# First solve of a delta-rule and mixture kernel: beta over squared norms, first evictions on two engines, and idle products cut from 18 long to 46 short

## The chip, the cores and the metric

The kernel runs on one core of one Trainium2 chip. The metric is device time in microseconds (us) of one execution, as the median of several. Durations of single instructions are in nanoseconds (ns) where so marked. The engines are TensorE (PE, with its weight loads as a row of its own, PEld), VectorE (DVE), ScalarE (ACT), GpSimd (POOL) and SyncE (SP, which issues most of the DMAs).

## The reference

For each of 4 x 8 heads a 48 x 48 state is carried over 768 positions. The output of that, as rows of 384, goes through a two-layer product with a clipped square between the layers.

```python
k_n = k / (np.linalg.norm(k, axis=-1, keepdims=True) + 1e-06)
for t in range(S):
    kt, vt, bt = (k_n[:, :, t], v[:, :, t], beta[:, :, t, None])
    y[:, :, t] = np.einsum('bhd,bhde->bhe', q[:, :, t], state)
    v_old = np.einsum('bhde,bhd->bhe', state, kt)
    state = state + bt[:, :, :, None] * np.einsum('bhd,bhe->bhde', kt, vt - v_old)
...
h = x @ w_in
g = np.where(h >= 1, h, np.where(h <= -1, 0.0, (h + 1) ** 2 / 4))
out = g @ w_out
```

## The kernel before, in words

The 768 positions are cut into 12 chunks of 64. Two chunks make a stage G. Inside a chunk the recurrence becomes a triangular system, so each stage needs the products of keys with keys (Gram matrices), the norms of the keys, the inverse of a triangular matrix (the solve), and then a chain of products that carries the state.

The chunks of stage 0 come first, and nothing can be overlapped with an earlier stage there: this is the front. Lines 679 to 713 write its order out by hand. `gram_k(g)` (L231) makes the Gram matrices of chunk g in two PSUM banks (L237) and returns its eviction, which copies the two banks to SBUF (L241). `lanes(G)` (L298) is a generator whose steps are run one at a time: two steps copy 32-column blocks side by side (L304, and L306 for stage 1), one step transposes them on DVE so that each partition holds one small system (L317), one step makes the norms and `gm` = beta / norm^2 (L319 to L327), and one multiplies the matrix by `gm` (L338) and transposes the norms (L340). `norms` (L277) takes a square root on ACT (L281) and does a Newton step on DVE (L282 to L285); `gm` then takes a reciprocal and two multiplications (L322 to L324). `solve(0)` (L343) is 15 steps of a multiplication and a subtraction on DVE (L355, L357). `unlanes(0)` (L386) multiplies by `gm` and transposes back (L391, L394, L396) into the tile XT. `scale_v` (L288) multiplies the values by the norms (L292).

PE meanwhile runs what it can: `place_beta` (L151, one product at L153), the key-query products (`gram_q`, L250), the Gram matrices of chunks 3 and 2, and between them products of a tile of zeros that nobody reads (`dense`, L163; L165). `dense(IDLE)` at L690 is the last of these: 18 products of 512 columns in the type fp32r, just ahead of the second `place_beta` (L705) and of `merge16_a` (L401, products at L405, evicted by ACT at L412), which needs the XT of `unlanes(0)`. Then come `merge16_b` (L419, subtracted and transposed by DVE at L424 and L425), `merge32` (L436, then L451 on ACT, L438, L443 on ACT), and the chain: `chain_u` (L508), `chain_y` (L539, L541; evicted at L556 and L561) and `chain_d` (L607). `stage` (L647) takes the strings in FRONT (L30), which put other work between: F one idle product, A and D steps of unpacking weights on ACT (L189, L205) and DVE (L195, L201, L208), L a step of `lanes(1)`, s a step of `scale_v(0)`, w a weight load (L124).

From L861 on a loop over (stage, weight tile) runs the two large products (`up`, L738, and `down`, L753), with the work of later stages between them.

All products of the type fp32 show as two weight loads and two products each in the trace; those of type fp32r show as one of each.

Of the kernel before, what the change touches and what calls it, by code (L numbers as in the profile page):

```python
# [7 lines left out]
F32 = mybir.dt.float32  # L8
F32R = mybir.dt.float32r
I32 = mybir.dt.int32  # L10
AF = mybir.ActivationFunctionType
ALU = mybir.AluOpType
# [7 lines left out]
DF = 2048  # L20
FT = DF // 128
WARM = 8
IDLE = 18
DENSE = (8, 4, 8, 10)
HALF = 6
PASSES = ((0, 0), (0, 1), (1, 0))
# [14 lines left out]
def delta_rule_moe(ctx: ExitStack, tc: tile.TileContext, kqa, kqb, kv, beta, w, out):  # L41
# [14 lines left out]
    nc = tc.nc  # L56
# [5 lines left out]
    P = 128  # L62
# [4 lines left out]
    sb = ctx.enter_context(tc.tile_pool(name="sb", bufs=2))  # L67
# [3 lines left out]
    K, KE, GE, Q, KV, XB, RAW, WT = {}, {}, {}, {}, {}, {}, {}, {}  # L71
# [9 lines left out]
    def half(x):  # L81
        return slice(x * H, x * H + H)
# [46 lines left out]
    beta_sb = const.tile([P, NS, 32], F32, name="beta_sb")  # L129
# [16 lines left out]
    for c0, base, step, n in ((0, -H, -C, NP), (NP, -C - H - NP, C, NP), (C, -C, C, H)):  # L146
        x = perm[:, 0:C].rearrange("c (a f l) -> c a f l", f=2, l=H)[:, :, :, c0:c0 + NP] if c0 < C else perm[:, C:P].rearrange("c (a f l) -> c a f l", f=2, l=H)
# [3 lines left out]
    def place_beta(n0, n1):  # L151
        b_ps = ps.tile([P, NS, 32], F32, **acc())
        nc.tensor.matmul(b_ps[:, n0:n1], perm, beta_sb[:, n0:n1], start=True, stop=True)  # L153

        def evict():
            nc.scalar.copy(out=beta_sb[:, n0:n1], in_=b_ps[:, n0:n1])
        return evict

    warm = sb.tile([P, 512], F32R, name="wx")
    nc.vector.memset(warm.bitcast(F32), 0.0)  # L160
    warm_ps = ps.tile([P, 512], F32, name="o1")

    def dense(n):  # L163
        for _ in range(n):
            nc.tensor.matmul(warm_ps, warm[:, 0:P], warm, start=True, stop=True)  # L165
    dense(WARM)
    mask = const.tile([P, C], F32, name="mask")
    nc.gpsimd.memset(mask, 1.0)
# [5 lines left out]
    tiny = const.tile([P, 1], F32, name="tiny")  # L174
# [4 lines left out]
    GG = const.tile([P, 2, NU, C], F32, name="GG")  # L179
# [42 lines left out]
    def quarters():  # L222
        return [(e, x) for e in range(2) for x in range(2)]

    def banks(*shape):
        return [ps.tile([P, H, *shape], F32, **acc()) for _ in range(2)]
# [4 lines left out]
    def gram_k(g):  # L231

        x, b_ = KE.pop(g) if g in KE else K[g], banks(C)
        for j in range(H):
            for e, f in quarters():
                k, o = x[f * C:f * C + D, e * H + j, :], (1 - e) * C
                nc.tensor.matmul(b_[f][o:o + C, j], k, k, start=True, stop=True)  # L237

        def evict():
            for f in range(2):  # L240
                nc.scalar.copy(out=(GE[g - 2] if g in (2, 3) else GG[:, g % 2])[:, half(f)], in_=b_[f])  # L241
        return evict

    def gram_q(g):
# [29 lines left out]
            return (raw, masks(True)) if g < 2 else lambda: run(masks()) if g < 4 else later()  # L274
        return evict

    def norms(n, out):  # L277

        y = sb.tile([P, 32], F32, name="y0")
        r = sb.tile([P, 32], F32, name="r1")  # L280
        nc.scalar.activation(out=y, in_=n, func=AF.Sqrt, bias=tiny)  # L281
        nc.vector.reciprocal(out=r, in_=y)  # L282
        nc.vector.tensor_tensor(out=r, in0=r, in1=n, op=ALU.mult)
        nc.vector.tensor_tensor(out=r, in0=r, in1=y, op=ALU.add)
        nc.vector.tensor_scalar(out=out, in0=r, scalar1=0.5, scalar2=1e-6, op0=ALU.mult, op1=ALU.add)  # L285
        return r

    def scale_v(g):  # L288

        for f in range(2):  # L290
            v, u = KV[g][:, 1, half(f)], g % 2 * NU + f * H
            nc.vector.tensor_tensor(out=v, in0=v, in1=S["N", g // 2][:, u:u + H, None].broadcast_to([P, H, D]), op=ALU.mult)  # L292
            yield

    S = {}
    ZT = XT[:, :, :, 0:32]

    def lanes(G):  # L298

        for g in range(2):  # L300
            x = GE[g] if G == 1 else GG[:, g]
            for u in (half(0), half(1)) if (G, g) == (0, 1) else (slice(0, NU),):
                for r in (0, C):
                    (nc.scalar.copy if G else nc.vector.tensor_copy)(out=x[r:r + 32, u, 32:64], in_=x[r:r + 32, u, 0:32])  # L304
            if G == 1:
                nc.scalar.copy(out=GD[:, g], in_=x[:, :, 32:64])  # L306
            yield
        A = S["A"] = sb.tile([P, 32, 32], F32, name="A", bufs=1)
        if G < WHOLE:
            X = S["X"] = sb.tile([P, 2, 16, 16], F32, name="X", bufs=1)  # L310
            Xf = X.rearrange("l s c t -> l (s c t)")
            nc.gpsimd.memset(X, 0.0)
            for s in range(2):
                nc.gpsimd.memset(Xf[:, 256 * s:256 * s + 256:17], 1.0)
        if G == 0:
            nc.gpsimd.memset(ZT[:, :, :, 16:32], 0.0)
        nc.vector.transpose(out=A, in_=(GD if G == 1 else GG[:, :, :, 32:64]).rearrange("p g u t -> p t (g u)"))  # L317
        yield
        n = sb.tile([P, 32], F32, name="N2")  # L319
        r = norms(A.rearrange("l j t -> l (j t)")[:, 0:1024:33], n)  # L320
        gm = S["gm"] = sb.tile([P, 32], F32, name="gm")
        nc.vector.reciprocal(out=r, in_=n)  # L322
        nc.vector.tensor_tensor(out=gm, in0=r, in1=beta_sb[:, G, :], op=ALU.mult)
        nc.vector.tensor_tensor(out=gm, in0=gm, in1=r, op=ALU.mult)  # L324
        N = S["N", G] = sb.tile([P, 32], F32, name="N3")
        if G:
            nc.vector.transpose(out=N, in_=n)  # L327
        yield
        if G >= WHOLE:
            nc.vector.scalar_tensor_tensor(out=A, in0=A, scalar=-1.0, in1=gm[:, :, None].broadcast_to([P, 32, 32]), op0=ALU.mult, op1=ALU.mult)  # L330
            nc.gpsimd.affine_select(out=A, in_=A, pattern=[[-1, 32], [1, 32]], base=0, channel_multiplier=0,  # L331
                                    compare_op=ALU.is_gt, fill=0.0)
            nc.gpsimd.memset(A.rearrange("l c t -> l (c t)")[:, 0:1024:33], 1.0)
            return
        A16 = S["A16"] = sb.tile([P, 2, 16, 16], F32, name="A16", bufs=1)
        for s in range(2):
            b = slice(16 * s, 16 * s + 16)
            nc.vector.tensor_tensor(out=A16[:, s], in0=A[:, b, b], in1=gm[:, b, None].broadcast_to([P, 16, 16]), op=ALU.mult)  # L338
        if G == 0:
            nc.vector.transpose(out=N, in_=n)  # L340
        yield

    def solve(G):  # L343

        X, A16 = S["X"], S["A16"]
        X32 = S["X32"] = sb.tile([P, 32, 32], F32, name="A", bufs=1)
        if G:
            for b in range(2):
                nc.scalar.copy(out=X32[:, 16 * b:16 * b + 16], in_=warm.bitcast(F32).rearrange("p (u t) -> p u t", t=32))
        else:  # L350
            nc.gpsimd.memset(X32, 0.0)
        for j in range(15):
            n, m = j + 1, 15 - j
            pr = sb.tile([P, 240], F32, name="pr", bufs=1)[:, 0:2 * n * m].rearrange("l (s c t) -> l s c t", s=2, t=m)
            nc.vector.tensor_tensor(out=pr, in0=X[:, :, 0:n, j:j + 1].broadcast_to([P, 2, n, m]),  # L355
                                    in1=A16[:, :, j:j + 1, j + 1:16].broadcast_to([P, 2, n, m]), op=ALU.mult)
            nc.vector.tensor_tensor(out=X[:, :, 0:n, j + 1:16], in0=X[:, :, 0:n, j + 1:16], in1=pr, op=ALU.subtract)  # L357
            yield
# [27 lines left out]
    def unlanes(G):  # L386

        X, X32, gm = S["X"], S["X32"], S["gm"]
        for s in (1, 0):
            b = slice(16 * s, 16 * s + 16)  # L390
            nc.vector.tensor_tensor(out=X32[:, b, b], in0=X[:, s], in1=gm[:, None, b].broadcast_to([P, 16, 16]), op=ALU.mult)  # L391
            if G and s:
                nc.gpsimd.memset(ZT[:, :, :, 16:32], 0.0)
            nc.vector.transpose(out=XT[:, :, :, 32 + 16 * s:48 + 16 * s].rearrange("p g u t -> p t (g u)"), in_=X32[:, :, b].rearrange("l c t -> l t c"))  # L394
            yield
        nc.vector.transpose(out=ZT[:, :, :, 0:16].rearrange("p g u c -> p c (g u)"), in_=X32[:, 0:16, :])  # L396
        yield
# [244 lines left out]
    def run(gen, n=99):  # L642
        for _ in range(n):
            if next(gen, 0) == 0:
                break
# [37 lines left out]
    for g in range(2):  # L683
        dense(DENSE[g])
        raws.append(gram_q(g)())
    early = []
    for g in (3, 2):
        dense(DENSE[5 - g])
        early.append(gram_k(g))
    dense(IDLE)  # L690
    run(ln[0], 2)
    for x, r in enumerate(QS):
        for y in range(2):
# [7 lines left out]
    for x in (SF, SZ):  # L701
        nc.gpsimd.memset(x, 0.0)
    run(unlanes(0))
    one_ = lambda f, *a: [lambda: f(*a)]
    place_beta(1, NS)()  # L705
    stage(one_(merge16_a, 0), 0)
# [11 lines left out]
    items, first = [], {}  # L718
# [142 lines left out]
    for n, item in enumerate(items):  # L861
# [23 lines left out]
        if len(ready) == LAG:  # L885
            x = ready.pop(0)
# [12 lines left out]
    G = NS - 1  # L899
# [50 lines left out]
```

## Time and profile before

| | |
|---|---|
| Time, median of 3 runs | 591.02 us (589.74 to 594.14) |
| The profiled execution's own time | 590.3 us |
| Its span in the trace | 588.6 us, so 1.7 us lie around it |
| Mean granted clock of PE | 0.992 of full speed |
| PE products / weight loads in the trace | 569.0 us busy, x9585 / 493.3 us busy, x9585 |
| DVE / ACT busy | 405.2 us (69%) / 327.5 us (56%) |

The stated times run from the start of the span. "Idle before <-X" in a timeline names what ended the idle time of that engine; "issue" there means that the engine waited for nothing that the profile shows. In rows of stretches, the share after the engines is the granted clock of PE (1.00 is 2.4 GHz, 0.50 is 1.2 GHz), then the mean busy share of the DMA engines and the GB/s.

### The profile page before, as it was taken

The page shows a single profiled execution, that of the slowest core. Times are in us where ns is not written, and L with a number is a line of the kernel's source. Part 1 is how long each engine was busy: PE and PEld are TensorE (multiplying, and loading weights), DVE is VectorE, ACT ScalarE, POOL GpSimd, SP SyncE. Part 2 cuts the span into 40 slices and gives each one's busy share as a digit, 9 for nine tenths or more (in the row PEclk, how much of TensorE's full clock was granted, in tenths as well). Part 3 has the DMA queues.
Part 4 walks back from the last instruction along what each step waited for, and adds up shares of the span by engine and source line. Part 5 has one row for each costly group of instructions (what it writes and reads, how often), then busy time and mean ns, then how long its engine had stood idle before and what let it go on. Part 6 is the DMA issues. An engine that isn't in the chain of part 4 may idle for free.

```text
span 588.6 us, 21697 instructions
## 1 busy us (share of the span) xinstructions
PE 569.0 (97%) x9585; PEld 493.3 (84%) x9585; DVE 405.2 (69%) x828; ACT 327.5 (56%) x587; POOL 54.5 (9%) x91
## 2 busy tenths in 40 slices
PE   8998899999999999999999999999999999999996
PEld 7776788788978888888888888888888888898986
DVE  5977999963689864599954599954599955333332
ACT  4648886358644575545575445575445564454443
POOL 6200010000000500010400011300011300000000
PEclk9979999999999999999999999999999999999999
DMA  5673766200333111134011134011133000020001
GB/s 147 199 253 138 213 212 192 77 4 10 95 81 100 31 32 39 39 97 114 24 33 41 37 103 119 16 30 45 36 106 96 1 3 16 15 55 1 0 2 53
DMA packets 32302, 42.77 MB, mean 73 GB/s; under 512 B 7056, under 2 KB 26768, under 8 KB 32208
## 3 DMA queue, kind: packets, MB, share of 16 engines
q1 hardware_dynamic: 31216, 40.41, 24.0%
q8 instruction: 75, 1.23, 0.9%
q0 software_dynamic: 576, 0.57, 0.4%
q10 hardware_dynamic: 416, 0.39, 0.2%
q14 instruction: 19, 0.16, 0.1%
HBM read 34.47 MB, written 4.72 MB: 67 GB/s over the span
## 4 chain that ended last, share of the span: by engine, by line
PE 47%; issue 22%; DVE 14%; DMA 6%; SPq 6%; ACT 2%; POOL 1%; POOLq 0%; DVEq 0%; ACTq 0%
PE h L738 18%; PE o L753 17%; DMA wt<-in_w_dram 4%; PE ch L534 3%; PE ch L237 2%; DVE s L893 2%; PE ch L508 2%; DVE pr L366 1%; DVE A L368 1%; DVE glo L857 1%; PE ch L250 1%; SPq L595 1%; PE ch L492 1%; DMA KV<-in_kv_dram 1%; DVE wt L208 1%
## 5 line engine op out<-in xcount | busy, mean ns | idle before, releaser
L738 PE MATMUL h<-xb,wt 128*128 128x512 f32 (+1 forms) x918 | 223.0, 386 | 5.1 <-DVE s L893 2.0
L753 PE MATMUL o<-wt,ghi 128*128 128x384 f32 x768 | 200.0, 342 | 0.1
L738 PEld LDWEIGHTS h<-xb,wt 128*128 128x128 f32 x918 | 161.8, 188 | 38.9 <-DVE s L893 3.4
L753 PEld LDWEIGHTS o<-wt,ghi 128*128 128x128 f32 x768 | 137.2, 188 | 7.0 <-issue 0.3
L753 PE MATMUL o<-wt,glo 128*128 128x384 f32 x384 | 129.4, 337 | 0.4 <-DVE glo L857 0.4
L856 ACT CAST ghi<-s 128x512 fp32r<-128x512 f32 (+1 forms) x102 | 60.8, 597 | 120.4 <-DVE s L893 107.8
L893 DVE SCALAR_TENSOR_TENSOR s<-s,h 128x512 f32<-128x512 f32 (+1 forms) x102 | 66.3, 650 | 77.1 <-ACT s L891 76.8
L877 ACT ACTIVATE s<-h,half 128x512 f32<-128x512 f32 (+1 forms) x102 | 67.4, 661 | 53.8 <-PE h L738 53.6
L857 DVE TENSOR_TENSOR glo<-s,ghi 128x512 fp32r<-128x512 f32 (+1 forms) x102 | 66.8, 654 | 39.5 <-ACT ghi L856 39.3
L753 PEld LDWEIGHTS o<-wt,glo 128*128 128x128 f32 x384 | 72.1, 188 | 1.0 <-DVE glo L857 1.0
L891 ACT ACTIVATE s<-s 128x512 f32<-128x512 f32 (+1 forms) x102 | 62.2, 610 | 2.2
L368 DVE TENSOR_TENSOR A<-A,pr 128x30 f32<-128x30 f32 (+14 forms) x120 | 45.4, 378 | 4.4
L366 DVE TENSOR_TENSOR pr<-A 128x30 f32<-128x30 f32 (+14 forms) x120 | 43.4, 362 | 2.2
L272 POOL TENSOR_SCALAR_AFFINE_SELECT Q<-Q 64x512 f32<-64x512 f32 x32 | 21.7, 680 | 117.4 <-ACT Q L260 116.0
L165 PE MATMUL o<-wx 128*128 128x512 f32 x87 | 27.8, 464 | 1.5 <-DVE tiny L175 1.5
L534 PEld LDWEIGHTS ch<-Q,SU 64*64 64x64 f32 (+3 forms) x1056 | 22.4, 135 | 3.7 <-ACT ghi L856 1.5
L534 PE MATMUL ch<-Q,SU 64*64 64x64 f32 (+3 forms) x1056 | 24.7, 222 | 0.0
L331 POOL TENSOR_SCALAR_AFFINE_SELECT A<-A 128x1024 f32<-128x1024 f32 x4 | 5.6, 1390 | 191.5 <-DMA xb<-X 148.1
L165 PEld LDWEIGHTS o<-wx 128*128 128x128 f32 x87 | 18.2, 220 | 5.6 <-DVE tiny L175 1.5
L626 DVE TENSOR_TENSOR SU<-ch,SU 48x384 f32<-48x384 f32 x36 | 19.9, 554 | 3.9 <-PE ch L607 3.5
L590 DVE TENSOR_TENSOR X<-ch,X 128x128 fp32r<-128x128 f32 x20 | 5.8, 292 | 23.5 <-ACT xb L586 22.5
L517 ACT COPY SU<-ch 64x384 f32<-64x384 f32 (+1 forms) x30 | 14.3, 476 | 7.0 <-PE ch L508 6.7
(168 smaller groups left out, 559.5 us busy)
## 6 DMA issues: line engine op xcount, KB each, us to landing
wt<-in_w_dram SPq DMA_DIRECT2D x16, 768.0 KB, 5.6
out_dram<-wx SPq DMA_DIRECT2D x44, 96.0 KB, 2.2
KV<-in_kv_dram SPq DMA_DIRECT2D x36, 96.0 KB, 2.4
KV<-in_kv_dram SPq DMA_DIRECT2D x72, 48.0 KB, 2.3
KV<-in_kv_dram SPq DMA_DIRECT2D x12, 192.0 KB, 2.7
xb<-X SPq DMA_DIRECT2D x60, 32.0 KB, 2.0
K<-in_kqb_dram SPq DMA_DIRECT2D x12, 128.0 KB, 2.6
Q<-in_kqb_dram SPq DMA_DIRECT2D x12, 128.0 KB, 2.7
```

The source lines that it names most:

```text
L165: nc.tensor.matmul(warm_ps, warm[:, 0:P], warm, start=True, stop=True)
L272: nc.gpsimd.affine_select(out=y, in_=y, pattern=[[0, H], [1, C]], base=0, channel_multiplier=-1, compare_op=ALU.is_gt, fill=0.0)
L366: nc.vector.tensor_tensor(out=pr, in0=A[:, 0:n, j:j + 1].broadcast_to([P, n, m]), in1=A[:, j:j + 1, j + 1:32].broadcast_to([P, n, m]), op= ...
L368: nc.vector.tensor_tensor(out=A[:, 0:n, j + 1:32], in0=A[:, 0:n, j + 1:32], in1=pr, op=ALU.add)
L534: nc.tensor.matmul(yy[i][o * C:o * C + C, e, p], SF[rows, u:u + C], w_[rows, x, k, :], **how)
L738: nc.tensor.matmul(h[:, cols(bs)], WT[f][:, 0, x, k * P:(k + 1) * P], XB[G][:, y, k, cols(bs)], start=(n == 0), stop=(n == 8))
L753: nc.tensor.matmul(oacc[G, k], (ghi, glo)[x][:, k * P:(k + 1) * P], WT[f][:, 1, y, :], start=(new and n == 0), stop=(left[G, b] == 0 and n ...
L856: nc.scalar.copy(out=ghi[:, c], in_=s[:, c])
L857: nc.vector.tensor_tensor(out=glo[:, c], in0=s[:, c], in1=ghi[:, c], op=ALU.subtract)
L877: nc.scalar.activation(out=s[:, c], in_=h[:, c], func=AF.Relu, bias=mid, scale=0.5)
L891: nc.scalar.activation(out=s[:, c], in_=s[:, c], func=AF.Square)
L893: nc.vector.scalar_tensor_tensor(out=s[:, c], in0=s[:, c], scalar=1.0, in1=h[:, c], op0=ALU.min, op1=ALU.max)
```

## The change

Five edits, all in the front.

1. Stage 0 gets `squares` in place of `norms`: the square root still runs on ACT, but `gm` is beta / (n + 2e-6 y + 1e-12), with n the squared norm as it stands on the diagonal and y its root, without the Newton step. Two of its DVE instructions do not need the root (an addition to n, and a copy of n).
2. The Newton step moves into a helper `newton`. Stage 0 calls it in `norms_first`, after `unlanes(0)`, followed by the transpose of the norms that stood at L340.
3. The second bank of the Gram matrices of chunks 0 and 1 is evicted by DVE, the first still by ACT.
4. Of the side-by-side copies of chunk 1 (L304) the first half goes to ACT, the second stays on DVE.
5. `dense(IDLE)` becomes 46 products of 200 columns (9200 columns) in place of 18 of 512 (9216 columns).

```diff
-IDLE = 18
+IDLE = 46
...
-    def dense(n):
+    def dense(n, cols=512):
         for _ in range(n):
-            nc.tensor.matmul(warm_ps, warm[:, 0:P], warm, start=True, stop=True)
+            nc.tensor.matmul(warm_ps[:, 0:cols], warm[:, 0:P], warm[:, 0:cols], start=True, stop=True)
...
-                nc.scalar.copy(out=(GE[g - 2] if g in (2, 3) else GG[:, g % 2])[:, half(f)], in_=b_[f])
+                (nc.vector.tensor_copy if f and g < 2 else nc.scalar.copy)(out=(GE[g - 2] if g in (2, 3) else GG[:, g % 2])[:, half(f)], in_=b_[f])
...
-    def norms(n, out):
-
-        y = sb.tile([P, 32], F32, name="y0")
-        r = sb.tile([P, 32], F32, name="r1")
-        nc.scalar.activation(out=y, in_=n, func=AF.Sqrt, bias=tiny)
+    def newton(r, n, y, out):
         nc.vector.reciprocal(out=r, in_=y)
         nc.vector.tensor_tensor(out=r, in0=r, in1=n, op=ALU.mult)
         nc.vector.tensor_tensor(out=r, in0=r, in1=y, op=ALU.add)
         nc.vector.tensor_scalar(out=out, in0=r, scalar1=0.5, scalar2=1e-6, op0=ALU.mult, op1=ALU.add)
+
+    def norms(n, out):
+
+        y = sb.tile([P, 32], F32, name="y0")
+        r = sb.tile([P, 32], F32, name="r1")
+        nc.scalar.activation(out=y, in_=n, func=AF.Sqrt, bias=tiny)
+        newton(r, n, y, out)
         return r
+
+    def squares(n, gm, out):
+
+        y = sb.tile([P, 32], F32, name="y0")
+        d = sb.tile([P, 32], F32, name="r1")
+        nc.scalar.activation(out=y, in_=n, func=AF.Sqrt, bias=tiny)
+        nc.vector.tensor_scalar(out=gm, in0=n, scalar1=1e-12, scalar2=None, op0=ALU.add)
+        nc.vector.tensor_copy(out=d, in_=n)
+        nc.vector.scalar_tensor_tensor(out=gm, in0=y, scalar=2e-6, in1=gm, op0=ALU.mult, op1=ALU.add)
+        nc.vector.reciprocal(out=gm, in_=gm)
+        nc.vector.tensor_tensor(out=gm, in0=gm, in1=beta_sb[:, 0, :], op=ALU.mult)
+        S["first"] = y, d, out
...
-                    (nc.scalar.copy if G else nc.vector.tensor_copy)(out=x[r:r + 32, u, 32:64], in_=x[r:r + 32, u, 0:32])
+                    (nc.scalar.copy if G or u == half(0) else nc.vector.tensor_copy)(out=x[r:r + 32, u, 32:64], in_=x[r:r + 32, u, 0:32])
...
-        n = sb.tile([P, 32], F32, name="N2")
-        r = norms(A.rearrange("l j t -> l (j t)")[:, 0:1024:33], n)
-        gm = S["gm"] = sb.tile([P, 32], F32, name="gm")
-        nc.vector.reciprocal(out=r, in_=n)
-        nc.vector.tensor_tensor(out=gm, in0=r, in1=beta_sb[:, G, :], op=ALU.mult)
-        nc.vector.tensor_tensor(out=gm, in0=gm, in1=r, op=ALU.mult)
-        N = S["N", G] = sb.tile([P, 32], F32, name="N3")
-        if G:
+        if G == 0:
+            squares(diag, gm, n)
+        else:
+            r = norms(diag, n)
+            nc.vector.reciprocal(out=r, in_=n)
+            nc.vector.tensor_tensor(out=gm, in0=r, in1=beta_sb[:, G, :], op=ALU.mult)
+            nc.vector.tensor_tensor(out=gm, in0=gm, in1=r, op=ALU.mult)
             nc.vector.transpose(out=N, in_=n)
...
-        if G == 0:
-            nc.vector.transpose(out=N, in_=n)
         yield
+
+    def norms_first():
+
+        y, d, n = S["first"]
+        r = sb.tile([P, 32], F32, name="r1")
+        newton(r, d, y, n)
+        nc.vector.transpose(out=S["N", 0], in_=n)
...
-    dense(IDLE)
+    dense(IDLE, 200)
     run(ln[0], 2)
...
     run(unlanes(0))
+    norms_first()
```

The tiles N2, gm and N3 are made ahead of the transpose L317 instead of behind it.

## Rows read from the trace of the kernel before

**Rows 1.** Stretch of the steady loop: busy us of each engine, clock, DMA share, GB/s.

```profile
80.00:90.00 10.00, 10.00 (x107) 8.34 (x106) 9.90 (x20) 7.33 (x12) 0.00 (x0) 1.00 0.88 308
```

**Rows 2.** PE in the front, in order of time, 21 to 32 us.

```profile
21.57 4.38 PE L165 MATMUL o<-wx 128*128 128x512 f32 x18
...
26.15 1.26 PE L405 MATMUL ch<-XT,GG 32*32 32x16 f32 x128
27.34 0.50 PE L165 MATMUL o<-wx 128*128 128x512 f32 x1
28.60 0.43 PE L419 MATMUL ch<-wt,XT 32*32 32x16 f32 x28 [0.75 <-ACT wt L412]
30.29 1.57 PE L419 MATMUL ch<-wt,XT 32*32 32x16 f32 x100 [1.26 <-issue]
```

**Rows 3.** The same, from 33 us on: idle products, then the first merge32.

```profile
32.38 4.76 PE L165 MATMUL o<-wx 128*128 128x512 f32 x11
...
37.07 1.20 PE L436 MATMUL h<-XT,GG 32*32 32x32 f32 x64
```

**Rows 4.** Stretches of half a microsecond, where the granted clock changes (columns as rows 1).

```profile
30.00:30.50 0.50, 0.21 (x16) 0.22 (x20) 0.50 (x1) 0.00 (x0) 0.00 (x0) 0.52 0.71 135
...
36.50:37.00 0.50, 0.50 (x2) 0.06 (x1) 0.47 (x3) 0.00 (x0) 0.00 (x0) 0.65 1.04 257
```

**Rows 5.** ACT in order of time, around the first eviction that the solve feeds.

```profile
26.51 1.73 ACT L189 ACTIVATE xb<-wt 128x768 f32<-128x768 f32 x2
28.15 0.35 ACT L412 COPY wt<-ch 128x256 f32<-128x256 f32 x1
```

**Rows 6.** DVE in order of time, from the first copies to the solve.

```profile
7.96 2.24 DVE L304 COPY GG<-GG 32x512 f32<-32x512 f32 x6 [4.31 <-ACT GG L241]
10.23 2.01 DVE L317 STREAM_TRANSPOSE A<-GG 128x1024 f32<-128x1024 f32 x1
12.66 0.35 DVE L282 RECIPROCAL r<-y 128x32 f32<-128x32 f32 x1 [0.42 <-ACT y L281]
...
13.74 0.35 DVE L322 RECIPROCAL r<-N 128x32 f32<-128x32 f32 x1
...
14.58 0.76 DVE L338 TENSOR_TENSOR A<-A,gm 128x256 f32<-128x256 f32 x2
15.26 0.20 DVE L340 STREAM_TRANSPOSE N<-N 128x32 f32<-128x32 f32 x1
```

**Rows 7.** ACT's first eviction in order of time; then a DVE form up to 50 us (mean ns).

```profile
6.85 1.07 ACT L241 COPY GG<-ch 128x512 f32<-128x512 f32 x2 [2.59 <-PE ch L237]
...
L517 DVE COPY SU<-o 128x384 f32<-128x384 f32 x1 | 0.5, 547 | 0.0
```

**Rows 8.** DVE in order of time, behind the solve.

```profile
24.67 1.29 DVE L394 STREAM_TRANSPOSE XT<-A 128x512 f32<-128x512 f32 x1
...
28.30 0.54 DVE L292 TENSOR_TENSOR KV<-KV,N 128x384 f32<-128x384 f32 x1
...
34.12 0.42 DVE L424 TENSOR_TENSOR XT<-XT,ch 128x256 f32<-128x256 f32 x1
```

**Rows 9.** Weight loads in order of time: the idle products, then nine products of 256 columns.

```profile
21.57 3.95 PEld L165 LDWEIGHTS o<-wx 128*128 128x128 f32 x18
...
51.00 1.13 PEld L738 LDWEIGHTS h<-xb,wt 128*128 128x128 f32 x9 [1.09 <-ACT SU L621]
```

**Rows 10.** PE by form, whole span: a product of type fp32 (busy, mean ns).

```profile
L153 PE MATMUL o<-beta_sb,perm 128*128 128x160 f32 x2 | 0.4, 300 | 0.0
```

**Rows 11.** Stretches from the start to two gaps of PE: number of products, of weight loads.

```profile
0.00:28.98 28.98, 26.42 (x601) 20.92 (x601) 21.36 (x58) 15.25 (x28) 13.66 (x33) 1.00 0.61 174
0.00:46.60 46.60, 42.17 (x983) 33.21 (x984) 33.91 (x86) 23.88 (x43) 13.66 (x33) 0.93 0.68 211
```

**Rows 12.** Waits of PE up to 80 us: total, times, longest.

```profile
PE ch L539 <- issue: 1.5, 1, 1.5
```

**Rows 13.** DMA queues of the whole span: packets, MB, share.

```profile
q8 instruction: 75, 1.23, 0.9%
```

More of the change, by code (lines that the diff above doesn't have):

```diff
@@ L275, in gram_q @@
         return evict
+    def newton(r, n, y, out):
+        nc.vector.reciprocal(out=r, in_=y)
+        nc.vector.tensor_tensor(out=r, in0=r, in1=n, op=ALU.mult)
+        nc.vector.tensor_tensor(out=r, in0=r, in1=y, op=ALU.add)
+        nc.vector.tensor_scalar(out=out, in0=r, scalar1=0.5, scalar2=1e-6, op0=ALU.mult, op1=ALU.add)
     def norms(n, out):
@@ L281, in norms @@
         nc.scalar.activation(out=y, in_=n, func=AF.Sqrt, bias=tiny)
[L282 to L285, printed above, removed]
-        return r
+        newton(r, n, y, out)
+        return r
+    def squares(n, gm, out):
[8 more added lines that the diff above has]
+        S["first"] = y, d, out
     def scale_v(g):
@@ L316, in lanes @@
             nc.gpsimd.memset(ZT[:, :, :, 16:32], 0.0)
+        n = sb.tile([P, 32], F32, name="N2")
+        diag = A.rearrange("l j t -> l (j t)")[:, 0:1024:33]
+        gm = S["gm"] = sb.tile([P, 32], F32, name="gm")
+        N = S["N", G] = sb.tile([P, 32], F32, name="N3")
         nc.vector.transpose(out=A, in_=(GD if G == 1 else GG[:, :, :, 32:64]).rearrange("p g u t -> p t (g u)"))
         yield
-        n = sb.tile([P, 32], F32, name="N2")
-        r = norms(A.rearrange("l j t -> l (j t)")[:, 0:1024:33], n)
-        gm = S["gm"] = sb.tile([P, 32], F32, name="gm")
-        nc.vector.reciprocal(out=r, in_=n)
-        nc.vector.tensor_tensor(out=gm, in0=r, in1=beta_sb[:, G, :], op=ALU.mult)
-        nc.vector.tensor_tensor(out=gm, in0=gm, in1=r, op=ALU.mult)
-        N = S["N", G] = sb.tile([P, 32], F32, name="N3")
-        if G:
+        if G == 0:
[5 more added lines that the diff above has]
+            nc.vector.tensor_tensor(out=gm, in0=gm, in1=r, op=ALU.mult)
             nc.vector.transpose(out=N, in_=n)
```

## The prediction

> **What bounds the kernel now.** I read the busy shares by stretch first. From 80 us on PE is busy without a break [rows 1], so time won ahead of that point is kept if what follows simply starts earlier; the front, where all five edits lie, ends some 30 us before it. So I followed the front engine by engine, in order of time, and looked for what ends last at each hand-over.
>
> Up to 26 us DVE ends last: the solve runs without a break, XT's first half is transposed at 24.67 + 1.29 = 25.96 [rows 8], and merge16_a starts at 26.15, as the 18 idle products run out: they began at 21.57 and took 4.38 [rows 2]. Then it is no longer DVE. The eviction L412 waits until 28.15 behind two weight steps of ACT that began at 26.51 and took 1.73 [rows 5]. merge16_b starts at 28.60, does 28 of its 128 products and stands for 1.26 us waiting for nothing that the profile shows ("issue") [rows 2]. During that stand the clock falls to half (the mean of 30.00 to 30.50 is 0.52, so at about 30.0) and is back at about 36.85, since 36.50 to 37.00 averages 0.65 [rows 4]. The last 100 products of merge16_b take 1.57 us where 128 of the same kind in L405 took 1.26 [rows 2], and 11 idle products take 4.76 [rows 3] where 18 took 4.38. So merge32 starts only at 37.07 [rows 3], although DVE ended what it reads at 34.12 + 0.42 = 34.54 [rows 8]. In the front PE itself is last there, by 2.5 us, through one stall and one slow stretch.
>
> **The stall is a matter of position.** Until that stand PE has done 601 products with their 601 loads, 1202 instructions; until the next such stand (1.5 us, in L539 [rows 12]) 983 and 984, so 1967 [rows 11]. The difference is 765, three times 255. Queue q8 brings 75 portions [rows 13] for PE's 2 x 9585 = 19,170 instructions (the table), about 256 each. I take it that PE stands where a new portion begins and has not come. 46 products in place of 18 put 28 pairs ahead of it, and merge16_b had done just 28 pairs: the border moves to its first product, where PE waits for L412 anyway.
>
> The page "Runtime: NRT & Kernel Launch" of the Trainium skill, section "Instruction fetch mechanics", says that instructions come in blocks of 256 and that crossing a border costs little and is mostly hidden. The block size agrees with the 255 of rows 11; "mostly hidden" doesn't hold for the 1.26 and 1.5 us of rows 2 and 12, though it may hold for the borders between. By the rule the move is worth nothing, which is part of the second rival.
>
> **The change part by part.**
>
> *First evictions and copies.* DVE now starts at 6.85, beside ACT's first eviction [rows 7], in place of 7.96, behind it [rows 6]. It gets two evictions of 128x512 out of PSUM, for which before has no row: 0.55 for 384 columns [rows 7] is the lower end, the same in proportion to columns, 0.73, the upper; I take 0.7. It loses two of the four half-width copies in the L304 group; a full-width one counting as two at most, each is at least 2.24 / 8 = 0.28, so 1.68 of the group stays [rows 6]. 6.85 + 1.4 + 1.68 = 9.93 against 10.23 for the transpose: 0.3 us. Bounds: 0 (if ACT's half, two copies behind its own eviction, is late) to 0.6 (evictions at the lower end).
>
> *gm without Newton.* Before, the four Newton operations take 12.66 to 13.74, then a reciprocal and two multiplications 13.74 to 14.58 [rows 6]. After, the addition and the copy run while ACT makes the root, in the idle 0.42 us of the L282 row, and what stays is again three operations on 32 columns, one of them a reciprocal: 0.84. So 1.08 goes (0.9 if the two in front overrun the root), and L340's 0.20. The solve, and with it XT, come 0.3 + 1.08 + 0.2 = 1.6 us earlier: XT at 24.4.
>
> *The Newton step comes back.* Its four operations took 13.74 - 12.66 = 1.08 and the transpose 0.20 [rows 6], 1.28 in all, now on DVE between the last transpose and L292. So L292 and everything behind it in DVE's queue, L424 included, moves only 1.6 - 1.28 = 0.3 us: L424 ends at about 34.25 (it would be 1.6 earlier if the step could wait until later, and no earlier than before if 0.3 more is lost on the way). No DMA is issued or moved by any of the edits.
>
> *Idle products.* Loads start every (3.95 - 0.19) / 17 = 0.221 us at 512 columns and every (1.13 - 0.19) / 8 = 0.117 at 256 [rows 9], the last load estimated at 0.19. On that line 200 columns take 0.094. 46 of them take 4.3 where 18 took 4.0: merge16_a at about 26.4. Lower bound: in proportion to columns, 0.086, 4.0 us, no change. Upper bound: the fp32 products. One of 160 columns takes 300 ns in each of its two instructions [rows 10]; I read that as two passes (320 columns at 2.4 GHz, 133 ns) behind a start-up that the product ahead covers, an estimate. A short product charged four such passes of 200 columns would take 0.33 us, 15.3 in all. I take 0.094, nearest to the 256-column row of the same type; the other end is the third rival. So DVE's 1.6 us do not start merge16_a earlier: PE's own filling is late next. They matter in another way: with XT's wait met at 24.4 and short products in the queue, PE's reading of instructions can pass merge16_a's first products, and so ask for the next portion, while the idle products still run.
>
> *merge16_b.* It can start at 28.57 as before (L412 is ACT's) and run through in 1.26 to 1.6 us, if the portion is there. The border before the stand lies 127.5 pairs ahead of it, some 30 pairs into merge16_a, crossed at about 26.4; the portion was there at 30.28, 3.9 us later. Asked for at 24.4 to 26.4 it comes at 28.3 to 30.3. I take an end at 30.4 in place of 31.86: 1.4 us; bounds 0 and 2.0.
>
> *The twelve idle products and merge32.* If the clock falls again, these take 12 x 0.43 = 5.1 us, and merge32 starts at 35.5; if it stays, 12 x 0.22 = 2.7 us, and DVE is late next: 34.4. I take 35.0, a gain of 2.1; bounds 0 and 2.7. The wait that PE ends there is DVE's L424, with merge32's products and ACT's L451 behind it.
>
> *The second stand* in L539 sits 28 pairs earlier; the portion is asked for during L438 rather than L508, so some of its 1.5 us may go, but the next portion is then needed sooner, with the weight loads filling the DMA engines. I take 0.2; bounds -0.5 and 1.5. The later borders move by 28 pairs each; without a row for them I take 0, with 0.7 either way.
>
> Sum: 2.1 + 0.2 = 2.3 us off 590.3, the profiled execution's own time, so 588.0. The median of the runs is 0.7 above that execution, so 588.7 on its scale; I say 588.6.
>
> **The rivals.**
>
> *More than this:* the clock stays (2.7), the second stand goes whole (1.5) and the later borders help (0.7): 4.9, about 586. For it: the gaps are few and sit at borders. Against: the next portion only comes due sooner.
>
> *Hidden:* the portion is asked for no earlier, merge16_b starts at 30 and ends at 31.9 as before, the clock falls as before. The shorter path to the solve then does not do what it says, for PE or ACT is late next at each hand-over. ACT's L412 and DVE's 1.28 us that come back speak for it: 590.5, give or take 1.
>
> *Slower:* the short products are charged like fp32 ones, 0.33 us. The idle products then end at 36.9, merge16_a runs to 38.4, merge16_b from about 39.0 to 40.3, twelve idle products at full clock to 43.1: merge32 6.0 late, less up to 1.5 at the second stand. 596 on the scale of the median. It decides from 0.2 us each on: idle end E + 6.3 (merge16_a 1.5, eviction 0.7, merge16_b 1.3, twelve idle products 2.8) passes 37.07 at E = 30.8, (30.8 - 21.57) / 46. For it: no fp32r row has fewer than 256 columns. Against: 512 and 256 columns lie on one line through nearly zero, with no sign of a step [rows 9].
>
> **How the numbers follow.** Forecast (gain of 1 to 4) 0.55, hidden 0.23, more 0.10, slower 0.12. The forecast's own range is 587 to 590. The range for 8 in 10 takes in most of the larger gain and the hidden case with the scatter of the runs (589.74 to 594.14), but not the slower one: 585.2 to 593.5. One per cent, 5.9 us, is about what a measurement of this kernel can tell from no change. Only the top of the larger gain with scatter passes it downward (0.06), only the upper part of the slower case upward (0.06): within it 0.88.
>
> **What would show it.** Right: the solve's first product near 13.9, XT's first half done near 24.4, L292 near 28.0; 46 loads 0.09 us apart; merge16_b's 128 products in one piece; merge32 before 36; gaps of PE at pair counts 28 lower in the old order. Wrong: a gap in front of merge16_b up to 30 us, half clock up to merge32, or idle products past 28 us.

## The result, and the profile after

The kernel became slower: a median of 597.63 us in 16 runs (594.31 to 602.87) against 591.53 in 16 runs of before, a ratio of 1.0105 with a 95% interval of 1.0082 to 1.0129. The profiled execution took 597.92 us, 7.6 more than that of before, so it can be read for the loss. 588.6 was forecast, and the range ended at 593.5. Ratios leave out runs that came over 1.5% above the fastest of their kernel: one of twelve in "rest, 92", "rest, 16" and "before, 92" below, three of twelve in "late move".

**Where the time went.** A stand, below, is a time in which PE does nothing; a pair is a product with its weight load; a portion is the 255 instructions that come at once, 127.5 pairs, and a border is where the next portion begins. PE does the same 9,498 products in the same order in both kernels if the idle ones are left aside. For each I took its start after, less its start before. The difference is a running account:

| where (time of before) | 50 us | 70 us | 105 us | 140 us | 250 us | end |
|---|---|---|---|---|---|---|
| after less before, us | -0.16 | +2.31 | +2.27 | +6.49 | +7.45 | +7.57 |

Two short stretches hold most of it: 2.5 us between 50 and 70, and 4.2 between 105 and 140. The front, where all the edits lie, ends level in this execution, though not without events. PE there, in order of time, as [rows 2, 3] (start, us, line, operation, tiles, count, wait ahead of it):

```profile
20.69 5.39 PE L165 MATMUL o<-wx 128*128 128x200 f32 x46
...
26.30 1.26 PE L428 MATMUL ch<-XT,GG 32*32 32x16 f32 x128
...
28.86 1.26 PE L442 MATMUL ch<-wt,XT 32*32 32x16 f32 x128 [0.88 <-DVE N L364]
33.69 5.05 PE L165 MATMUL o<-wx 128*128 128x512 f32 x12 [3.56 <-issue]
38.67 0.50 PE L459 MATMUL h<-XT,GG 32*32 32x32 f32 x20
```

merge16_b (now L442) runs in one piece and ends at 30.12 where it ended at 31.86. But PE then stands for 3.56 us in front of the idle products, waiting for nothing that the profile shows, and the first merge32 (L459) begins at 38.67 in place of 37.07. That is 1.6 us lost. It comes back by 50 us, because the stand of 1.5 us in `chain_y` [rows 12] is gone.

DVE's path is shorter, as meant (same columns; [rows 6, 8]):

```profile
7.33 0.69 DVE L241 COPY GG<-ch 128x512 f32<-128x512 f32 x1 [3.69 <-PE ch L237]
...
10.43 2.02 DVE L336 STREAM_TRANSPOSE A<-GG 128x1024 f32<-128x1024 f32 x1
...
14.57 0.19 DVE L378 TENSOR_TENSOR pr<-X,A 128x30 f32<-128x30 f32 x1
...
23.77 1.29 DVE L417 STREAM_TRANSPOSE XT<-A 128x512 f32<-128x512 f32 x1
...
28.67 0.56 DVE L307 TENSOR_TENSOR KV<-KV,N 128x384 f32<-128x384 f32 x1
```

The two places of the loss, far behind the edits. First a merge16_a (the piece "a1" of the list PIECES), then a merge16_b (the piece "b2"):

```profile
52.09 1.23 PE L428 MATMUL ch<-XT,GG 32*32 32x16 f32 x125
54.90 0.23 PE L428 MATMUL ch<-XT,GG 32*32 32x16 f32 x3 [1.58 <-issue]
55.07 2.88 PE L165 MATMUL o<-wx 128*128 128x512 f32 x6
...
121.48 1.23 PE L442 MATMUL ch<-A,XT 32*32 32x16 f32 x125
124.31 0.29 PE L442 MATMUL ch<-A,XT 32*32 32x16 f32 x3 [1.60 <-issue]
```

And the same two in the kernel before:

```profile
52.26 1.26 PE L405 MATMUL ch<-XT,GG 32*32 32x16 f32 x128
53.45 1.66 PE L165 MATMUL o<-wx 128*128 128x512 f32 x6
...
118.64 1.26 PE L419 MATMUL ch<-A,XT 32*32 32x16 f32 x128
119.83 0.62 PE L753 MATMUL o<-wt,ghi 128*128 128x384 f32 x2
```

Each group of 128 short products went through in one piece before; after, it stops three products before its end. What follows runs at half the granted clock: the six idle products take 2.88 us where they took 1.66.

The 2.5 us between 50 and 70 are not that stand alone. When the six idle products are done PE is 2.8 us behind; 1.3 of that come back, as stands of 0.25 and 0.83 us at 55.84 and 59.56 in the kernel before (borders too) have no counterpart; and about as much goes again around the next merge32, where PE waits longer for DVE (after, then before) and the clock is at half from 65.4 to 68.8 us:

```profile
64.52 1.35 PE L459 MATMUL ch<-XT,GG 32*32 32x32 f32 x64 [1.49 <-DVE XT L447]
...
62.00 1.20 PE L436 MATMUL ch<-XT,GG 32*32 32x32 f32 x64 [0.53 <-DVE XT L424]
```

For the second place, the stretches of 118 to 130 us (busy us and counts of PE, PEld, DVE, ACT, POOL, then the granted clock, DMA share, GB/s), before:

```profile
118.00:124.00 6.00, 6.00 (x210) 5.11 (x209) 5.28 (x9) 3.41 (x6) 1.04 (x2) 1.00 0.03 6
124.00:130.00 6.00, 6.00 (x174) 5.08 (x177) 3.05 (x5) 3.58 (x6) 0.00 (x0) 1.00 0.01 3
```

and after:

```profile
118.00:124.00 6.00, 3.85 (x140) 2.66 (x134) 4.42 (x7) 4.46 (x8) 1.55 (x3) 0.95 0.17 40
124.00:130.00 6.00, 5.69 (x63) 5.22 (x67) 1.70 (x3) 0.62 (x1) 0.52 (x1) 0.50 0.01 3
```

Here a stand of 1.6 us costs about as much again and more in the half clock behind it: 63 products in the second stretch where before did 174.

**What PE waits for in these stands.** Queue q8 brings the instructions [rows 13], and the trace has a start and a duration for each of its packets. One answer holds a whole packet: DMA of the changed kernel, 121.7 to 123.1 us, by queue.

```profile
DMA packets 1, 0.02 MB, mean 12 GB/s; under 512 B 0, under 2 KB 0, under 8 KB 0
## 3 DMA queue, kind: packets, MB, share of 16 engines
q8 instruction: 1, 0.02, 5.8%
```

That packet starts at 121.72 and ends at 123.02, and PE goes on at 124.31, 1.29 us later. Nothing else is moved in that time. In the profiles of the fourteen kernels of this study there are 54 places within a few instructions of a multiple of 255, counted from the stand of [rows 2, 11], where one instruction of PE starts over 0.8 us after the one ahead; in 50 of them PE goes on 1.2 to 1.6 us after the end of a q8 packet, in the other four 1.9 to 4.0 us after. From 300 us on the count drifts by 22 to 32 instructions, and six more stands show there at the drifted place, each ending 1.3 to 1.6 us after a packet. With that drift allowed for, none of the 1,041 borders in the fourteen profiles is crossed before its packet has ended. So the prediction's reading of the border is seen directly. A packet takes 0.9 to 1.7 us, mostly 1.1. In places without other DMA traffic it usually starts about 1.1 us (0.4 to 1.7) after PE has crossed the border before. Together with the 1.4 us behind it that is 3.6 us: PE then gets its next 255 instructions 3.0 to 4.0 us after it went over the last border, and a portion that PE eats faster ends in a stand. The packet does not always start behind the border: at some places in the front and from 300 us on it starts with it or up to about 0.6 us ahead of it, and such stands end 2.1 to 2.7 us after the last border.

### The profile page after: what moved, and what is told of

Same layout as the page of the kernel before. It is cut to its first block, busy times and chain, and to the rows that moved or that the text cites. A ratio compares the mean times of both kernels' runs of the same rounds, so it can differ in the third digit from the quotient of the medians.

```text
span 596.2 us, 21758 instructions
## 1 busy us (share of the span) xinstructions
PE 573.0 (96%) x9613; PEld 497.4 (83%) x9613; DVE 406.3 (68%) x830; ACT 327.7 (55%) x587; POOL 54.3 (9%) x91
## 4 chain that ended last, share of the span: by engine, by line
PE 52%; issue 23%; DVE 15%; DMA 4%; SPq 2%; ACT 2%; POOL 1%; POOLq 0%; DVEq 0%; ACTq 0%
PE h L762 18%; PE o L777 17%; PE ch L557 3%; DMA wt<-in_w_dram 3%; PE o L165 2%; PE ch L237 2%; DVE pr L389 2%; DVE A L391 2%; PE ch L531 1%; PE ch L515 1%; PE ch L250 1%; DVE glo L881 1%; DVE s L917 1%; DVE SU L649 1%; SPq L618 1%
## 5 line engine op out<-in xcount | busy, mean ns | idle before, releaser
L777 PEld LDWEIGHTS o<-wt,ghi 128*128 128x128 f32 x768 | 138.8, 190 | 6.9
L901 ACT ACTIVATE s<-h,half 128x512 f32<-128x512 f32 (+1 forms) x102 | 67.4, 660 | 56.9 <-PE h L762 56.8
L165 PE MATMUL o<-wx 128*128 128x512 f32 (+1 forms) x115 | 30.0, 410 | 5.1 <-issue 3.6
L165 PEld LDWEIGHTS o<-wx 128*128 128x128 f32 x115 | 20.8, 220 | 8.9 <-issue 3.7
```

Source lines behind the costliest of these rows:

```text
L165: nc.tensor.matmul(warm_ps[:, 0:cols], warm[:, 0:P], warm[:, 0:cols], start=True, stop=True)
L777: nc.tensor.matmul(oacc[G, k], (ghi, glo)[x][:, k * P:(k + 1) * P], WT[f][:, 1, y, :], start=(new and n == 0), stop=(left[G, b] == 0 and n ...
L901: nc.scalar.activation(out=s[:, c], in_=h[:, c], func=AF.Relu, bias=mid, scale=0.5)
```

## The experiments

Theory: the 28 added pairs move every later border, and at some of them a group of 128 short products now fills a portion; the portion is eaten in some 1.3 us, PE stands, and the clock falls. Rivals: the short products themselves, or the moved work of DVE and ACT. The account of each run, made like that above (profiled execution less that of before, us), with the ratio of times to before:

| run | moved by (pairs) | ratio [95%] | at 50 us | 50 to 70 | 105 to 140 | end |
|---|---|---|---|---|---|---|
| the change | 28 | 1.0105 [1.0082, 1.0129] | -0.2 | +2.5 | **+4.2** | +7.6 |
| short idle only | 28 | 1.0130 [1.0089, 1.0172] | -1.6 | +5.0 | **+2.3** | +5.9 |
| rest only | 0 | 0.9974 [0.9950, 0.9998] | -0.7 | -0.1 | -0.7 | -1.1 |
| same place, long | 28 | 1.0099 [1.0070, 1.0129] | -0.1 | +1.5 | **+2.6** | +4.5 |
| whole portion | 128 | 1.0033 [1.0002, 1.0064] | +2.3 | -0.2 | -0.8 | +1.0 |
| rest, 92 | 92 | 1.0013 [0.9986, 1.0040] | +2.6 | +1.5 | -0.7 | +3.3 |
| rest, 16 | 16 | 1.0012 [0.9987, 1.0038] | +0.1 | -0.6 | +0.2 | -0.1 |
| rest, 64 | 64 | 1.0041 [1.0020, 1.0063] | +2.9 | +2.7 | -0.6 | +4.8 |
| before, 92 | 92 | 0.9985 [0.9952, 1.0018] | -1.3 | +2.9 | -0.8 | +0.9 |
| six ahead | 28 | 1.0136 [1.0103, 1.0169] | +4.0 | +0.9 | **+2.9** | +7.9 |
| back in step | 28, from 61 us on 128 | 1.0118 [1.0081, 1.0156] | +2.4 | +5.2 | -0.2 | +6.7 |
| both local | 28, from 61 us on 128 | 1.0146 [1.0115, 1.0177] | +2.6 | +4.4 | -0.1 | +7.3 |
| late move | 0, from 58 us on 28 | 1.0056 [1.0025, 1.0086] | -3.6 | +5.0 | **+1.3** | +5.3 |

**One part alone.** First each half of the change by itself.

```diff
  short idle only, against before:
-IDLE = 18
+IDLE = 46
-    dense(IDLE)
+    dense(IDLE, 200)
  rest only, against the change:
-    dense(IDLE, 200)
+    dense(18)
```

> The kernel before with only the idle products changed: 46 of 200 columns in place of 18 of 512. Position theory (PE's instruction portions begin 28 pairs earlier in the program, and at two or three places a whole portion then holds short products alone): slower than before by 5 to 8 us, with stands of about 1.6 us near the end of stage 1's first 128-product groups. Rival (the loss comes from the later Newton step or from the two-engine evictions on DVE): within 1.5 us of before. Second rival (short products themselves keep the clock down or run too long): a loss, but only in the front, up to 40 us.

> The changed kernel with 18 idle products of 512 columns, as before: evictions on two engines, squares, later Newton step alone. Position theory: stands of PE at the same pair counts as before, time within 1.5 us of before (at best 1 us faster). Rival (DVE's later Newton step or the evictions): slower by 5 to 7 us.

The idle products alone give the whole loss: 1.0130, whose interval holds the 1.0105 of the change. PE stands at the same two places, three products before the end (PE of "short idle only", in order of time):

```profile
55.89 0.29 PE L405 MATMUL ch<-XT,GG 32*32 32x16 f32 x3 [1.44 <-issue]
...
122.08 1.23 PE L419 MATMUL ch<-A,XT 32*32 32x16 f32 x125
124.71 0.29 PE L419 MATMUL ch<-A,XT 32*32 32x16 f32 x3 [1.40 <-issue]
```

The other edits alone are at most a small gain, 0.9974, some 1.5 us. With the other edits alone PE stands where it stood before (PE of "rest only" in order of time, to compare with [rows 2, 3]), and merge32 comes half a us earlier, at 36.60:

```profile
28.15 0.43 PE L442 MATMUL ch<-wt,XT 32*32 32x16 f32 x28 [0.79 <-ACT wt L435]
29.79 1.47 PE L442 MATMUL ch<-wt,XT 32*32 32x16 f32 x100 [1.20 <-issue]
...
36.60 1.27 PE L459 MATMUL h<-XT,GG 32*32 32x32 f32 x64
```

**The count or the shortness?** The 18 long idle products again, with 28 pairs that cost almost nothing: fp32 products of 32 by 32 by 16 into the idle bank (two pairs each). Then 128 pairs more than before, which is one whole portion and so puts the later borders back.

```diff
+    def tiny_idle(n):
+        x = warm.bitcast(F32)
+        for j in range(n):
+            r = j % 4 * 32
+            nc.tensor.matmul(warm_ps[r:r + 32, 0:16], x[r:r + 32, 0:32], x[r:r + 32, 0:16], start=True, stop=True)
  same place, long:
-    dense(IDLE, 200)
+    dense(18)
+    tiny_idle(14)
  whole portion:
-    dense(IDLE, 200)
+    dense(14)
+    tiny_idle(66)
```

> The changed kernel with 18 idle products of 512 columns followed by 28 pairs of 32x32 products of 16 columns, so as many pairs as the changed kernel and the same positions, but long idle products. Position theory: as slow as the changed kernel, 5 to 8 us over before, with the same stands. Rival (short idle products themselves): within 1.5 us of before.

> The changed kernel with 14 idle products of 512 columns followed by 132 pairs of 32x32 products of 16 columns, so 128 pairs more than before: one whole portion of 256 instructions. Position theory: the portions begin where they began before, so the time is back within 2 us of before although it has 100 pairs more than the changed kernel. Rival (more instructions in the front cost as such): at least as slow as the changed kernel.

The first loses what the change loses (1.0099) with no product of 200 columns in it; its 28 tiny pairs are short too, but take 0.4 us in all. Its front in PE's order of time, merge16_b and the stand behind it:

```profile
29.33 1.26 PE L447 MATMUL ch<-wt,XT 32*32 32x16 f32 x128 [1.50 <-DVE KV L312]
34.43 3.89 PE L165 MATMUL o<-wx 128*128 128x512 f32 x10 [3.84 <-issue]
```

The second, "whole portion", lost a third of that. Its account is level from 50 us on, as a whole portion should make it; its 2.3 us in front are of its own making, since the 132 tiny pairs fill a portion themselves. Two stands follow (the same view of this second kernel):

```profile
24.37 1.29 PE L170 MATMUL o<-wx 32*32 32x16 f32 x132
...
26.29 0.43 PE L433 MATMUL ch<-XT,GG 32*32 32x16 f32 x29
28.96 1.29 PE L433 MATMUL ch<-XT,GG 32*32 32x16 f32 x99 [2.24 <-issue]
...
35.30 1.57 PE L447 MATMUL ch<-wt,XT 32*32 32x16 f32 x100 [3.78 <-issue]
```

**Other moves, by a model that failed.** I then took the time between two borders from the trace of before, called 3.9 us less that time the stand, and added the stands up for every move: 11.2 us for 16 pairs, 6.1 for 64, 1.5 for 92, 6.4 as it is. Four kernels tested it.

```diff
  rest, 92 (and the same two edits in the kernel before: before, 92):
-        dense(DENSE[g])
+        dense(DENSE[g] - 1)
+        tiny_idle(12)
...
-        dense(DENSE[5 - g])
+        dense(DENSE[5 - g] - 1)
+        tiny_idle(12)
...
  rest, 16 (behind the 18 long products):
+    tiny_idle(8)
  rest, 64 (behind each of the four earlier groups):
+        tiny_idle(8)
```

> The three DVE and ACT edits with 18 idle products of 512 columns, and 92 pairs more ahead of the first solve: in each of the four earlier idle groups one product of 512 columns less and 24 pairs of 32x32 products of 16 columns more. Sum over the whole trace of (3.9 us less the time from one portion's begin to the next), where that is positive: 6.4 us at the borders of the run with the three edits alone, 1.5 us with the borders moved by 92. Position theory: 3 to 7 us faster than before, though the front has 92 pairs more. Rival (only the front's own order counts, later borders don't): within 2 us of before.

> The three edits with 18 idle products of 512 columns, followed by 16 pairs of 32x32 products of 16 columns (0.2 us). The sum of shortfalls is 11.2 us at a move of 16, against 6.4 at none and 11.0 at 28. Position theory: about as slow as the changed kernel, 4 to 8 us over before. Rival (the loss needs just the 28 of the change, where a whole portion is one group of products): within 2 us of before.

> The three edits with 18 idle products, and 64 pairs more, 16 in each of the four earlier idle groups. The sum of shortfalls is 6.1 us, as at no move (6.4). Position theory: within 2 us of the run with the three edits alone, so 3 us under to 1 us over before. Rival (every added pair costs): slower than with 16 pairs added.

> The kernel before with the same 92 pairs added as in the run with a move of 92, and nothing else. Position theory: 3 to 6 us faster than before, without any of the change's edits. Rival (the gain of that other run comes from the three edits, once the positions don't hide it): within 1 us of before.

All four missed: none is clearly faster, and 16 loses nothing that can be measured. The rivals' ranges held instead for 92 (twice) and 16; for 64 the sign of the rival did, though its interval overlaps that of 16, and the price does not go by the number of pairs, since 92 cost no more. The model adds up stands as if each moved the end, and leaves out that a stand changes the time to the next border. The table shows both: kernels that are 1 to 4 us ahead at 50 us give that and more back by 70 ("late move", "short idle only", "before, 92"). There, in the kernel before, five borders in a row are crossed at 48.2, 52.5, 55.8, 59.6 and 63.1 us, 3.4 to 4.3 us apart. That is close to the pace at which portions come, so a lead in front can turn into standing there; that this is where these leads went is argued, not shown.

**The two places by themselves.** First the six idle products are put ahead of "a1", so that its portion is no longer all short products; then 100 pairs are added behind it, so that 28 + 100 make one portion (127.5) and half a pair, and all later borders are back where before has them; then both; and last the 28 pairs not in front but there.

```diff
  six ahead:
-PIECES = ((1, "a1 f6 r1"), (3, "b1"),
+PIECES = ((1, "f6 a1 r1"), (3, "b1"),
  back in step ("t" is tiny_idle):
+PIECES = ((1, "a1 f6 r1 t25"), (2, "t25"), (3, "b1"),
  both local:
+PIECES = ((1, "f6 a1 r1 t25"), (2, "t25"), (3, "b1"),
  late move:
-    dense(IDLE, 200)
+    dense(18)
...
+PIECES = ((1, "a1 f6 r1 t14"), (3, "b1"),
```

> The changed kernel, with the six idle products of stage 1 issued ahead of its merge16_a and no longer behind it: the same instructions, none moved past the 134 that are exchanged, every other border where the changed kernel has it. The portion from pair 1111 to 1238.5 then holds six 512-column products besides short ones and takes PE some 1.3 us longer. Theory (a stand is the time to fetch the next portion less the time that PE takes for the present one, here and nowhere else): the stand of 1.58 us at pair 1238 falls to 0.3 or goes, the half-clock stretch of 55.0 to 58.5 us with it, and of the 2.3 us that were lost there 1.5 to 2.3 come back: 595.3, 594.5 to 596.2, ratio to before about 1.007. The stand at pair 2642 stays at 1.3 to 1.7 us with its half clock. Rival (the stand comes of where the border lies, whatever the portion holds): a stand of 1.5 us at pair 1238, now within merge16_a six products further back, and 597.6.

> The changed kernel, with 100 pairs of tiny idle products added behind stage 1's r1 piece (50 there, 50 half an item later): 28 + 100 is 127.5 and half a pair, so from there on every border lies where the kernel before has it, while the borders up to pair 1366 lie where the changed kernel has them. Theory: the stand at pair 1238 stays (1.6 us, half clock, 2.3 us lost), the one at old pair 2642 goes with its half clock, and its 4.4 us come back, less 1.0 for the added products: 594.2, 593 to 595.5, ratio about 1.005. Rival (the loss beyond 100 us is not of borders): 598.6, with the clock at half from 124 us on as in the changed kernel.

> Both at once: the six idle products ahead of merge16_a, and the 100 pairs behind r1. Theory: neither stand of over 1 us at pairs 1238 and 2642 is left, and of the 6.7 us some 6 come back, less 1.0 for the added products: 592.2, 591 to 593.5, ratio 1.002, though the stand at pair 729 in front (3.6 us) is still there. Rival (the stand in front, with its moved place, is what costs): 597 to 598.

> The changed kernel with the 18 long idle products of before in front, so that the borders up to pair 1366 lie as before, and 28 pairs of tiny products behind stage 1's r1 piece, so that every later border lies as in the changed kernel. Theory: no stand at pair 729 or 1238; a stand of 1.3 to 1.7 us at pair 2642 with half clock behind it, and 4.4 us lost there and 0.3 in the added products: 594.0, 592.8 to 595.2, ratio 1.0075. Rival (the move must be made in front to cost): 589.5 to 590.

As times, the first three missed: 599.22, 598.04 and 599.78 us, none better than the change. At the two places they did what the theory says. With six ahead, "a1" runs whole, with no stand and at full clock, and the account grows by 0.9 between 50 and 70 in place of 2.5, while "b2" still stands. (The longer portion is not the only difference at "a1": the packet starts 0.1 us ahead of its border there, and 0.85 behind it in the change.) PE of that kernel, in order of time:

```profile
56.12 1.55 PE L165 MATMUL o<-wx 128*128 128x512 f32 x6
57.60 1.26 PE L428 MATMUL ch<-XT,GG 32*32 32x16 f32 x128
...
124.05 1.23 PE L442 MATMUL ch<-A,XT 32*32 32x16 f32 x125
126.61 0.28 PE L442 MATMUL ch<-A,XT 32*32 32x16 f32 x3 [1.33 <-issue]
```

Back in step, "b2" is whole and the clock behind it full; nothing is lost between 105 and 140 (the same view of this kernel):

```profile
126.21 1.26 PE L447 MATMUL ch<-A,XT 32*32 32x16 f32 x128
127.40 0.62 PE L782 MATMUL o<-wt,ghi 128*128 128x384 f32 x2
```

What I had mis-sized is the tool and the front. The 100 tiny pairs, priced at 1.0 us, cost 2.7 (5.2 - 2.5) and 3.5 (4.4 - 0.9): they are short products too, and in "back in step" they bring stands of 1.4 and 1.5 us at 64.5 and 69.6 us, with half clock from 66.5 to 76.7. And up to 50 us these three kernels are the changed kernel, instruction for instruction; their fronts lose 4.0, 2.4 and 2.6 us in the profiled executions where that of the change lost nothing. The stand behind merge16_b was 3.6 us in one and 4.9, 5.5 and 4.1 in the others. So the level front of the one execution that I had may have been a lucky draw; with one execution of each, and these three taken in another set of runs, that is not shown.

The late move took 593.8 us in the runs counted, as forecast (595.45 over all twelve, 0.3 above its range): moving the borders by 28 pairs only behind 58 us makes half the loss without moving a border in the front. The stand at "b2" is back, in PE's order of time:

```profile
120.27 1.23 PE L447 MATMUL ch<-A,XT 32*32 32x16 f32 x125
123.10 0.23 PE L447 MATMUL ch<-A,XT 32*32 32x16 f32 x3 [1.60 <-issue]
```

But only 1.3 us of its loss are made there, not the 4.4 expected: the clock stayed full. In this execution 5.0 go between 50 and 70 us, where a lead of 3.6 us runs out. Most of that, 3.2 us, is gone ahead of the 28 tiny pairs: PE stands 25 products into "a1", at a border that has not been moved, and the clock is at half from 50.4 to 67.4 us (PE of this kernel):

```profile
50.28 1.55 PE L433 MATMUL ch<-XT,GG 32*32 32x16 f32 x103 [1.26 <-issue]
51.76 2.93 PE L165 MATMUL o<-wx 128*128 128x512 f32 x6
...
304.81 0.22 PE L507 MATMUL ch<-GG 32*32 32x32 f32 x2 [1.57 <-issue]
```

Another 2.9 us go between 300 and 400, at the stand in the last line, which ends 1.3 us after a packet, and with a half clock from 306.4 to 309.8. So the stretch that holds the stand at "b2" cost 1.3 us with the clock full and 4.2 in the change with it at half; and the median of the late move cannot be put down to "b2" alone.

Read down the column "105 to 140" of the table: every kernel whose borders there are moved by 28 pairs loses 1.3 to 4.2 us; the eight with another move lie between -0.8 and +0.2. That, with the packet ahead of each stand, is what shows the cause. How the 6 us of the median divide among the places is not shown: each account is of one execution. The lowest ratio is that of "rest only", the change without its idle products: 0.9974, whose interval just leaves out 1, as one of twelve can by chance.

**What the clock adds.** Over all executions, not the profiled one alone: the 16 of the change have a mean granted clock of 0.9829, 75 of before, taken with the experiments, 0.9896, with median spans of 595.9 and 588.7 us. A share of (1 - 0.9829) x 2 of the span at half clock is some 20.4 us a run, against 12.3: 8 us more, worth up to 4 us of work. The rest, at least 3 of these 7.2 us or 2 of the 6.1 between the medians of the result, is then the stands themselves. That split is worked out, not measured.

## Why the prediction was wrong, step by step

Most steps of the front came out.

- *Evictions, gm, L340.* From DVE's first eviction to the solve 14.57 - 7.33 = 7.24 us; the prediction had 13.9 - 6.85 = 7.05. An eviction took 0.69 (0.7 taken). gm is ready 1.25 us after the transpose where it took 2.34, a gain of 1.09 (1.08). In this execution everything is 0.5 late, since the first Gram products ended later than in before: XT's first half is done at 25.06 rather than 24.4.
- *Newton behind the solve.* 27.43 to 28.67, 1.24 us (1.28 taken). DVE's last step before merge32 starts at 34.53, 0.4 later than in before, with the 0.5 that this execution is late. Right.
- *Idle products.* The pitch is 0.112 us, not 0.094 (weight loads of the changed kernel, in order of time, as [rows 9]):

```profile
20.69 5.21 PEld L165 LDWEIGHTS o<-wx 128*128 128x128 f32 x46
```

  It is (5.21 - 0.19) / 45, and that is nearly what 256 columns cost [rows 9], so the line through 512 and 256 columns doesn't go on below; the rival that priced them at 0.33 is refuted. merge16_a began at 26.30 (26.4 forecast) only because the idle products could start 0.9 us earlier.
- *merge16_b.* One piece, its end at 30.12 (30.4). Right, and for the reason given: the border moved to its first product. The packet ended at 27.51 and PE went at 28.86, 1.35 later, so part of the 0.88 us that the profile puts down to DVE may be the border too.
- *The twelve idle products and merge32: the step that failed first.* 35.0 was forecast, 38.67 measured, and the clock was at half from 31.2 to 38.1 us, as long as before. The prediction moved one border and didn't ask about the next. In before the portion behind the stand held 100 short products, the twelve idle ones and the first of merge32; after, it is merge16_b whole, 1.26 us of work, and the packet started at 31.50 only. The stand was not removed but put behind merge16_b and grew from 1.26 to 3.56 us.
- *The second stand* went whole, 1.7 us at that place where 0.2 was taken (1.5 was the bound).
- *"The later borders move by 28 pairs each; without a row for them I take 0, with 0.7 either way"*: this is the term that made the result. It measured +2.5 and +4.2 us in the profiled execution, and some 0.9 more further on. The rows for it were there. The count of pairs up to each group of 128 short products can be read from the trace of before: 1,085 to 1,213 for "a1" and 2,489 to 2,617 for "b2". The borders lie at 601 + 127.5 k, so at 1,111, 1,238.5, 2,513.5 and 2,641. Add 28 to the groups, and both fill a portion to within four pairs. Before, each had one border inside it. So the term that was put at nothing for want of a row is the step that failed: moved borders turned two groups into whole portions, 6.7 us in this execution with what followed at each.

The rival on the slower side had the right sign and the wrong mechanism (the price of short products). The rule of the Trainium skill that the prediction weighed (page "Runtime: NRT & Kernel Launch", section "Instruction fetch mechanics": crossing a border is mostly hidden) holds for most borders of this trace, as 75 packets stand against 3 gaps of over 0.8 us before and 4 after. Its exceptions decided the case.

Two things stay open. Why the packet comes later in the front wasn't tried: ahead of the stands behind merge16_b it starts up to 4.4 us after the border, with the DMA share near 1.00 between 31 and 37 us, which suggests that it waits among the loads. And the account by place is of single executions; the front alone differs by 4 us between executions of kernels that are the same up to there.

## What to carry to other kernels

An edit that changes the number of instructions on PE moves every later border of the instruction fetch, so idle products are not free even where they are hidden: before adding some, list the groups of short instructions by their count and see which would fill a portion. Lengthen idle work by columns rather than by count, or add a whole portion, and not of short products (the one tried here was of short ones and still lost 0.3%; one of long products wasn't tried). And a single profiled execution can show a stretch as level that loses 2 to 4 us in the profiles of kernels with the same front: where a stand depends on a transfer, look at several.

## What the runs showed of the hardware that was not expected

- The instruction portions are visible one by one as packets of q8. On nearly idle DMA engines the loop from border to border is 3.0 to 4.0 us: some 1.1 until the packet starts, 0.9 to 1.7 for its 16 KB, and 1.2 to 1.6 from its end to the first instruction. At three of the five borders between 48 and 63 us of the kernel before (48.2, 55.8 and 59.6) PE stands, for 1.5, 0.25 and 0.8 us, and the profile names no engine that it waits for.
- A product of 200 columns cost 0.112 us with its weight load, against 0.117 for 256 and 0.221 for 512.
- A stand of 1.6 us ("b2") was followed by 6.8 us at half clock, 123.4 to 130.2, though PE worked without a break from 124.3 on; in the late move a stand of the same length at the same place was followed by none.
